# Windowed attention and an affine ResMLP on one core: another order of the first steps

## The chip, the cores and the metric

The kernel runs on one core of a Trainium2 chip. The metric is device time in microseconds (us), lower is better; before the change the median of three runs is 258.79 us (256.25 to 259.25).

## The reference

Two parts follow each other, on float32 inputs. Attention with batch 4, 8 heads, 768 positions, head size 64: a query sees the first 4 positions (sinks) and the 128 latest. Its result is laid out as x (4, 768, 512) and goes through an affine MLP block:

```python
scores = scale * q @ k^T            # kept: sinks or 0 <= rel < 128
x   = softmax(scores) @ v           # heads side by side: (B, S, 512)
a1  = alpha1 * x + beta1
u   = x + lam * (w_tok @ a1)        # w_tok: 768 x 768, over positions
a2  = alpha2 * u + beta2
out = u + lam * (relu(a2 @ w_ch1) @ w_ch2)   # 512 -> 2048 -> 512
```

## The kernel before

The Python code does not issue instructions as it goes. It adds some 1143 small steps to a plan (`add`), each a closure that issues one or a few instructions on one engine. At the end `plan.emit(ORDER, ENGINES, HOMES, IDLES)` runs the steps in the order of the tuple ORDER; the digit string ENGINES gives each step's engine (0 ACT, 1 DVE, 2 PE, 3 POOL, 4 SP), HOMES gives each buffer's place in its pool, and IDLES puts filler matmuls on a zero tile ahead of a step (step, PSUM home, number). So ORDER sets the order on every engine and every DMA queue. Waits come from the data and buffers that instructions share; each engine takes its instructions in the order in which they were issued.

A batch goes through: loading q and k of head pairs, casting to 16 bits, transposing (for the first two batches on PE, L504 and L507, evicted by ACT or DVE, L155 and L157), scores (L617 and L681; for some tiles a bias matmul, L612 and L678, puts the mask in first), exp on ACT, masks on DVE or POOL, the product with v (L718, with the sinks' part at L604 and L711), the norm (L743, L744), then the token mixing (`tok`, L849), u (L856), its transposes (L890), the first matmul of the MLP in 32 groups of four matmuls per batch (`mlp1`, L929), relu (L935, L937), and the second matmul (L1114, or in batches 1 to 3 a Strassen form, L1046). Steps of the next batch's attention are mixed into the MLP of the one before.

What concerns the start:

- SP's queue (`load_qk` L397, `load_v0` L424, `load_wtok` L435) asks for w_tok's first tile, q and k of the first head pair, and then slices of v and further tiles of w_tok. The other head pairs of batch 0 come in as casting DMAs of POOL (L390, into 16 bits). w_ch1 comes in four quarters, also casting DMAs of POOL (`load_w1`, L448); SP has small copies that wait for a quarter (`gate`, L455).
- ScalarE's queue asks for alpha2 and beta2 (`ab_row`, L169, L170), and, after DVE has zeroed their tiles, for lam, alpha1 and beta1, four copies of each row (L192).
- `fold_rows` multiplies alpha1 and beta1 by lam (DVE, L1164), spreads the rows over the partitions with a shuffle (L1166), transposes `ab_row` on PE (`abT`, L1168) and copies it to `ab2`.
- POOL makes the constants: `make_iden` (L325, L326), `make_masks` (L333 to L341), `make_bm` (L358), `make_sel` (L365, L369); DVE makes the biases from the masks (L348). PE's transposes need the identity.
- `cast_wtok` casts a tile of w_tok with its row sums (DVE L816 or ACT L814), transposes it (L809) and evicts it to `wtokT`. `cast_v0` casts batch 0's v.
- POOL forms half products of x with lam*alpha1 (L753), the operand of `tok`.

Of the kernel before, what the change touches and what calls it, by code (L numbers as in the profile page):

```python
# [77 lines left out]
def kernel(  # L78
# [119 lines left out]
    for r in range(NR):  # L198
# [18 lines left out]
        26, 6, 9, 7, 10, 5, 11, 8, 18, 15, 72, 19, 1, 12, 3, 0, 4, 2, 22, 14, 73, 74, 45, 48, 46,  # L217
        17, 39, 49, 47, 53, 13, 40, 50, 41, 90, 95, 43, 91, 51, 54, 103, 52, 16, 44, 61, 104, 42,
        96, 109, 100, 62, 107, 110, 63, 55, 28, 108, 92, 56, 101, 21, 68, 65, 59, 93, 20, 69, 97,
        102, 111, 94, 24, 98, 57, 60, 30, 112, 105, 23, 58, 99, 113, 128, 106, 114, 116, 25, 131,  # L220
        135, 78, 115, 64, 27, 138, 31, 32, 117, 132, 29, 129, 136, 33, 122, 66, 125, 34, 123, 137,
        119, 139, 126, 35, 79, 70, 120, 140, 124, 84, 71, 80, 133, 130, 141, 67, 146, 85, 134, 121,
        147, 144, 75, 118, 158, 86, 154, 148, 159, 145, 142, 87, 149, 150, 155, 160, 143, 76, 88,
        151, 156, 81, 77, 166, 152, 162, 167, 89, 127, 82, 163, 213, 83, 168, 209, 164, 165, 214,
        210, 153, 217, 179, 211, 178, 157, 197, 229, 36, 212, 215, 218, 185, 216, 226, 230, 219,
        176, 161, 177, 220, 169, 223, 222, 232, 225, 224, 221, 227, 237, 233, 279, 238, 234, 228,
        273, 280, 182, 171, 204, 291, 274, 175, 289, 292, 200, 231, 293, 290, 246, 294, 295, 199,
        384, 241, 248, 188, 186, 257, 296, 247, 172, 243, 277, 174, 181, 242, 259, 258, 187, 170,
        278, 267, 37, 260, 271, 358, 268, 198, 285, 349, 272, 381, 301, 286, 366, 351, 303, 302,
        189, 297, 378, 173, 304, 281, 180, 352, 203, 249, 190, 282, 298, 379, 250, 287, 380, 192,  # L230
        353, 385, 288, 206, 283, 386, 369, 375, 367, 265, 284, 368, 202, 370, 266, 363, 376, 371,
        253, 377, 201, 299, 254, 372, 364, 183, 382, 191, 300, 373, 615, 365, 275, 374, 383, 357,
        261, 276, 408, 262, 387, 263, 184, 409, 205, 195, 239, 411, 264, 410, 395, 269, 396, 240,
        397, 270, 196, 388, 614, 621, 235, 412, 400, 194, 244, 398, 236, 401, 255, 617, 251, 245,
        256, 389, 390, 399, 252, 311, 359, 207, 193, 391, 424, 616, 335, 425, 393, 341, 426, 392,
        336, 648, 427, 634, 413, 394, 312, 636, 414, 428, 419, 404, 420, 415, 360, 405, 313, 429,
        208, 422, 337, 416, 361, 441, 421, 622, 402, 314, 423, 442, 626, 403, 305, 638, 315, 406,
        430, 640, 316, 435, 431, 306, 641, 355, 436, 443, 619, 437, 338, 649, 618, 438, 362, 317,
        432, 637, 407, 307, 433, 345, 444, 339, 439, 635, 318, 445, 450, 434, 639, 644, 319, 451,
        628, 452, 620, 440, 308, 645, 340, 453, 417, 446, 323, 447, 418, 320, 309, 448, 324, 321,  # L240
        658, 322, 329, 449, 642, 659, 454, 325, 625, 643, 330, 646, 347, 455, 326, 623, 343, 647,
        464, 344, 456, 465, 348, 466, 460, 457, 467, 650, 327, 458, 331, 461, 629, 459, 472, 462,
        632, 463, 653, 356, 651, 656, 627, 332, 38, 654, 480, 333, 342, 624, 652, 473, 310, 476,
        468, 471, 470, 469, 481, 474, 488, 885, 477, 475, 482, 492, 655, 490, 493, 350, 483, 478,
        514, 491, 516, 489, 657, 479, 515, 660, 517, 630, 882, 665, 518, 663, 354, 328, 666, 502,
        880, 661, 664, 498, 879, 519, 508, 499, 346, 503, 678, 662, 512, 509, 679, 504, 513, 487,
        484, 671, 485, 676, 486, 506, 677, 877, 548, 505, 672, 680, 507, 526, 549, 546, 527, 631,
        334, 522, 674, 681, 528, 547, 907, 523, 534, 903, 529, 633, 682, 675, 878, 542, 683, 535,
        890, 689, 543, 550, 685, 684, 690, 510, 551, 494, 511, 673, 667, 544, 495, 668, 891, 496,
        686, 545, 901, 687, 669, 497, 693, 888, 688, 883, 530, 694, 670, 700, 531, 524, 897, 701,  # L250
        698, 500, 691, 525, 696, 699, 552, 501, 697, 704, 553, 558, 695, 705, 904, 692, 562, 559,
        706, 909, 887, 707, 563, 564, 898, 708, 702, 566, 565, 910, 715, 703, 567, 532, 716, 889,
        713, 533, 709, 714, 896, 520, 710, 556, 717, 521, 538, 557, 537, 540, 539, 536, 560, 541,
        899, 718, 921, 572, 922, 881, 711, 574, 884, 573, 576, 712, 561, 719, 902, 577, 575, 555,
        727, 720, 569, 908, 721, 580, 728, 578, 722, 581, 729, 554, 723, 905, 730, 568, 739, 724,
        579, 725, 592, 570, 911, 726, 582, 740, 593, 588, 912, 583, 595, 584, 571, 906, 743, 589,
        731, 585, 900, 590, 732, 605, 744, 587, 733, 596, 606, 734, 607, 611, 594, 597, 602, 745,
        612, 586, 613, 599, 895, 603, 591, 757, 765, 600, 758, 601, 759, 766, 741, 771, 760, 742,
        916, 772, 751, 917, 746, 773, 752, 913, 761, 919, 774, 886, 767, 918, 604, 762, 763, 598,
        768, 777, 764, 779, 920, 923, 780, 914, 755, 915, 778, 608, 756, 926, 930, 735, 609, 931,  # L260
        924, 927, 781, 736, 925, 775, 782, 737, 928, 753, 929, 893, 738, 934, 754, 892, 769, 935,
        932, 610, 941, 770, 819, 776, 942, 894, 939, 820, 821, 940, 937, 936, 823, 749, 822, 945,
        748, 824, 938, 747, 827, 933, 948, 950, 750, 952, 943, 951, 825, 953, 787, 828, 944, 807,
        788, 797, 826, 808, 949, 946, 829, 798, 801, 954, 830, 791, 802, 956, 947, 792, 783, 955,
        957, 963, 961, 784, 789, 958, 962, 811, 790, 964, 959, 785, 812, 965, 805, 786, 795, 806,
        960, 967, 796, 799, 793, 968, 966, 970, 972, 794, 813, 971, 969, 815, 973, 814, 809, 800,
        816, 803, 810, 974, 978, 804, 976, 979, 837, 975, 977, 835, 838, 980, 841, 836, 839, 842,
        818, 843, 840, 845, 981, 832, 982, 846, 817, 986, 844, 831, 990, 987, 983, 988, 847, 991,
        984, 851, 833, 992, 1002, 993, 834, 848, 855, 852, 985, 849, 1003, 859, 856, 1004, 989,
        1006, 850, 860, 1005, 853, 998, 1007, 1008, 868, 999, 857, 1009, 997, 865, 995, 858, 862,  # L270
        996, 869, 866, 1000, 874, 994, 854, 1001, 1016, 863, 875, 1040, 1017, 1038, 1041, 1032,
        1039, 871, 1020, 872, 1028, 1021, 1011, 1024, 1029, 1013, 1018, 1033, 1012, 1025, 1034,
        1019, 1036, 1010, 1035, 1042, 1037, 1076, 1043, 1070, 1077, 870, 1074, 1071, 1054, 1075,
        1022, 1055, 1060, 1023, 1048, 1061, 1058, 1049, 1066, 1059, 1014, 1044, 1015, 1067, 1072,
        1045, 1056, 1073, 1026, 1057, 1078, 1068, 1079, 1064, 1069, 1046, 1027, 1050, 1063, 1047,
        1052, 1082, 1053, 1051, 1084, 1083, 1062, 1065, 1030, 1085, 1080, 1101, 1031, 1081, 1091,
        1102, 1107, 1092, 1097, 1093, 1103, 864, 1108, 1105, 867, 1098, 1111, 1106, 1104, 1113,
        1112, 1089, 1114, 1115, 1086, 1116, 1090, 861, 1094, 1087, 1117, 1099, 1109, 1100, 1121,
        1095, 1110, 1125, 1118, 1122, 1124, 1134, 1126, 1123, 1128, 1135, 1127, 1119, 1136, 1088,
        1140, 1120, 873, 876, 1131, 1129, 1141, 1096, 1137, 1142, 1132, 1130, 1133, 1138, 1139,  # L280
    )
    ENGINES = (
        "3313134433443333444444444444444433334441111201201202120212021213030121211201211210200200"
        "2020201202011202020202020213213213213213213202002020202020213121312131213121312131404444"
        "4044413314433334411114413334444042213221321021020121021021321202020020211212021212120212"
        "1212020202120202120212020212020202020212122221022221422221022221422221022221013111111131"
        "1311333333302002002102132002132002102020101212010321213120301212131201012121312010121213"
        "1203212131212131213421342104110121042104213401012020202021202020212120202020212120202121"
        "2121202111202021202120202011202121212121111121212121212121132111213121421021421421421044"
# [1033 lines left out]
```

The softmax here doesn't subtract the row's maximum and nothing guards it: scores larger than these inputs give would overflow.

## Time and profile before

The profiled execution has a span of 254.3 us from the first to the last instruction; its own run time is not given apart from the three runs.

| | us |
|---|---|
| runs: median (lowest to highest) | 258.79 (256.25 to 259.25) |
| span of the profiled execution | 254.3 |
| PE busy in it | 245.6 |
| first fillers on PE; first transposes; first scores | 1.06; 7.60; 11.19 |
| first `tok` matmul | 31.39 |
| first `mlp1` matmul | 39.83 |
| issue of w_ch1's four quarters on POOL | 20.96 to 24.0 |
| last matmul | 250.05 |

Busy time counts an engine's instructions from start to end; filler matmuls count as busy too. A time in brackets behind an instruction is how long its engine was idle before it, with what ended that. Engines and lines are named as above; DMA queue q1 is SP's, q10 ScalarE's, q0 POOL's.

### The profile page before, as it was taken

How to read it: one execution, taken by the hardware profiler on the slowest of the kernel's cores; microseconds unless marked ns; L12 is line 12 of the kernel's file. 1: busy time of each engine (PE TensorE's matmuls, PEld its weight loads, DVE VectorE, ACT ScalarE, POOL GpSimd, SP SyncE). 2: the span in 40 equal slices, each digit the busy share in tenths (PEclk: the TensorE clock that was granted, in tenths of full speed). 3: DMA queues.
4: the chain of work that ended last, by engine and by line, in shares of the span. 5: the costliest groups of instructions: out<-in, count | busy, mean ns of one | idle time of the engine just before them, and what ended most of it. 6: DMA issues, size and time to landing. Idle time of an engine off the chain costs nothing.

```text
span 254.3 us, 5499 instructions
## 1 busy us (share of the span) xinstructions
PE 245.6 (97%) x2167; PEld 159.9 (63%) x2167; DVE 190.7 (75%) x402; ACT 133.2 (52%) x219; POOL 103.2 (41%) x124
## 2 busy tenths in 40 slices
PE   7799997999999999999999999999999999999993
PEld 7554644666555544566687686667667676667882
DVE  5688986767888874978879995578778983228892
ACT  2599913879977034787833434566660235543000
POOL 8318845876455527515782040065662120000010
PEclk9999999999999999999999999999999999999998
DMA  6999999899999999998484764520000140100327
GB/s 182 205 215 266 272 269 316 246 377 300 221 158 233 234 208 156 195 249 180 110 170 107 128 122 138 144 65 0 3 0 3 30 84 13 41 0 3 117 73 268
DMA packets 86129, 38.79 MB, mean 153 GB/s; under 512 B 73540, under 2 KB 80460, under 8 KB 86104
## 3 DMA queue, kind: packets, MB, share of 16 engines
q1 hardware_dynamic: 66576, 28.06, 47.3%
q10 hardware_dynamic: 15784, 7.11, 11.8%
q0 software_dynamic: 3744, 3.28, 8.0%
q8 instruction: 17, 0.28, 0.4%
q14 instruction: 8, 0.07, 0.1%
HBM read 29.91 MB, written 6.29 MB: 142 GB/s over the span
## 4 chain that ended last, share of the span: by engine, by line
PE 84%; DMA 11%; DVE 2%; POOL 1%; SPq 0%; issue 0%
PE h L929 32%; PE P L1046 22%; PE tok L849 9%; PE ch L1114 8%; DMA w1f<-in_moe_w_ch_dram 8%; PE pv L718 3%; PE S L617 3%; DMA nat<-in_k_dram 3%; PE tp L507 1%; POOL w1f L448 1%; PE tp L504 1%; DVE qkT L157 1%; DVE E L696 1%; PE pv L711 1%; PE pv L604 1%; PE idle L148 0%
## 5 line engine op out<-in xcount | busy, mean ns | idle before, releaser
L929 PE MATMUL h<-uT,w1f 128*128 128x384 f16 x512 | 89.8, 326 | 1.5 <-DMA w1f<-in_moe_w_ch_dram 1.5
L929 PEld LDWEIGHTS <-w1f 128*128 128x128 f16 x512 | 48.2, 98 | 32.7 <-DMA w1f<-in_moe_w_ch_dram 1.9
L935 ACT ACTIVATE hT<-h 128x384 f16<-128x384 f32 x77 | 37.0, 491 | 39.5 <-PE h L929 39.3
L937 DVE TENSOR_SCALAR hT<-h 128x384 f16<-128x384 f32 x51 | 27.8, 555 | 23.4 <-PE h L929 22.8
L1046 PEld LDWEIGHTS <-hT 128*128 128x128 f16 x408 | 39.5, 98 | 6.7 <-issue 0.2
L639 ACT ACTIVATE E<-S 128x1024 f16<-128x1024 f32 (+1 forms) x39 | 38.1, 1001 | 7.6 <-PE S L617 6.3
L762 POOL TENSOR_TENSOR tm<-x,la_b 128x512 f32<-128x512 f32 x18 | 24.3, 1353 | 24.2 <-DVE x L744 12.3
L849 PE MATMUL tok<-xh,wtokT 128*128 128x512 f16 x144 | 33.0, 379 | 0.0
L1059 DVE TENSOR_TENSOR x<-x,P 128x256 f32<-128x256 f32 x45 | 18.3, 419 | 11.3 <-PE P L1046 10.2
L1046 PE MATMUL P<-w2f,hT 128*128 128x256 f16 x216 | 26.5, 273 | 0.0
L849 PEld LDWEIGHTS <-wtokT 128*128 128x128 f16 x144 | 13.9, 98 | 15.0
L1114 PE MATMUL ch<-w2f,hT 128*128 128x512 f16 x96 | 23.2, 379 | 0.0
L1046 PE MATMUL P<-w2s,hT 128*128 128x256 f16 x192 | 23.1, 273 | 0.0
L1082 POOL TENSOR_TENSOR x<-x,pt 128x256 f32<-128x256 f32 x4 | 3.4, 854 | 47.5 <-DVE pt L1077 47.5
L155 ACT CAST u<-x 128x512 f16<-128x512 f32 x15 | 9.2, 615 | 24.9 <-DVE x L856 24.3
L744 DVE TENSOR_TENSOR x<-pv,rec 128x256 f32<-128x256 f32 x48 | 20.4, 425 | 1.7
L155 ACT CAST n<-nat 128x768 f16<-128x768 f32 x21 | 16.9, 828 | 8.9 <-DVE x L1125 6.4
L718 PEld LDWEIGHTS <-E 128*128 128x128 f16 x328 | 14.8, 98 | 5.1 <-issue 1.1
L856 DVE TENSOR_TENSOR x<-x,tok 128x512 f32<-128x512 f32 x24 | 16.0, 683 | 2.3 <-PE tok L849 2.3
L718 PE MATMUL pv<-vfs,E 128*128 128x65 f16 x328 | 17.7, 194 | 0.0
L579 POOL TENSOR_SCALAR_AFFINE_SELECT E<-E 128x512 f16<-128x512 f16 x12 | 7.5, 648 | 20.6 <-ACT E L639 20.6
L743 DVE RECIPROCAL rec<-pv 128x4 f32<-128x4 f32 x48 | 8.6, 179 | 7.2 <-PE pv L718 6.9
(134 smaller groups left out, 340.6 us busy)
## 6 DMA issues: line engine op xcount, KB each, us to landing
wst_w<-in_moe_w_ch_dram SPq DMA_DIRECT2D x8, 512.0 KB, 8.2
nat<-in_q_dram SPq DMA_DIRECT2D x10, 384.0 KB, 3.9
vnat<-in_v_dram SPq DMA_DIRECT2D x14, 256.0 KB, 5.7
nat<-in_k_dram SPq DMA_DIRECT2D x8, 384.0 KB, 7.2
out_dram<-x SPq DMA_DIRECT2D x11, 256.0 KB, 3.1
out_dram<-x ACTq DMA_DIRECT2D x10, 256.0 KB, 3.7
wtn<-in_moe_w_tok_dram SPq DMA_DIRECT2D x6, 384.0 KB, 4.1
w1f<-in_moe_w_ch_dram POOLq DMA_DIRECT2D x4, 512.0 KB, 15.4
```

Source lines behind the costliest of these rows:

```text
L155: nc.scalar.copy(o, i)
L639: nc.scalar.activation(eT.t, pS.t[:, :, 0 : n * w].rearrange("p e (i w) -> p e i w", i=n), AF.Exp, scale=scale)
L718: nc.tensor.matmul(po.t[:, hl, :], eT.t[:, e_, off + i, c : c + P], vf[j][:, h, :], start=(r < 2 and n == 0), stop=(n == len(parts) - 1 an ...
L744: nc.vector.tensor_mul(bx.t[:, 4 * G : 4 * G + 4, :], po.t[:, :, 0:D], rec.t.to_broadcast([P, 4, D]))
L762: engine[e].tensor_mul(bt.t, bx.t.rearrange("p h d -> p (h d)"), la1_b)
L849: nc.tensor.matmul(pt.t, wtokT[:, si, ti * P : (ti + 1) * P], hs[si].t, start=(si == 0), stop=(si == NR - 1))
L929: nc.tensor.matmul(ph.t, w1f[:, c, fi * P : (fi + 1) * P], bu.t[:, c, chk * NTOK : (chk + 1) * NTOK], start=(c == 0), stop=(c == NC - 1))
L935: nc.scalar.activation(bh.t[:, fi, :], ph.t, AF.Relu)
L937: nc.vector.tensor_scalar_max(bh.t[:, fi, :], ph.t, 0.0)
L1046: nc.tensor.matmul(pc.t, hh[:, nt * P : (nt + 1) * P], w(fi), start=(first and n_ == 0), stop=(n_ == HF - 1), skip_group_check=True)
L1059: nc.vector.tensor_add(row(bx)[:, cols], row(bx)[:, cols], pc.t)
L1114: nc.tensor.matmul(pc.t, bh.t[:, fi, nt * P : (nt + 1) * P], w2f[:, fi, :], start=(fi == 0), stop=(fi == NF - 1))
```

## The change

No step is added or removed, and no closure is altered: ORDER, ENGINES, HOMES and IDLES are replaced. Read as queues, batch 0's start changes thus:

- SP: q and k of the first pair go ahead of w_tok's first tile; the rest keeps its order.
- POOL: make_sel goes ahead of the first casting DMA; make_iden ahead of make_masks; make_bm behind the last two casting DMAs of q and k; w_ch1's first quarter goes directly behind the first v cast, the other three directly behind the second, all ahead of the first half product. POOL also gets two v casts (from ACT and DVE), and some half products change places.
- DVE: the product lam*beta1 comes first, then the casts of q and k, the product lam*alpha1, the copy to ab2 (from ACT), alpha1's shuffle, the biases, the eviction of the first k transposes (from ACT), the cast of w_tok's first tile, the eviction of the second pair's k (from ACT), the copy into vs, and the eviction of w_tok's first transposes (from ACT). beta1's shuffle comes later.
- ACT: evicts the second pair's q and the fourth pair's k (from DVE), and casts w_tok's tile 2 in place of tile 4.
- PE: abT first, then 52 fillers, transposes of q and k, the first two score tiles, transposes of the second pair's k, of w_tok's first tile, the third score tile, transposes of the second pair's q. Before: w_tok's transposes, those of q, k and the second pair's k, two score tiles, abT, the second pair's q, the third score tile.
- `mlp1` of batch 0, first half: before, the groups ran 1, 11, 8, 13, 12, 14, (uT transposes), 15, (uT transposes), 4, 10, 5; after, 1, 11, 8, 4, 10, 5, (both uT transposes), 15, 13, 14, 12. Groups 12 to 15 read w_ch1's last quarter, 4 to 7 its second, 8 to 11 its third.
- About a dozen steps behind that change engine (relu between ACT and DVE, casts of w_ch2 and sums between DVE and POOL), and some buffers change homes. Most of the order from batch 1 on is as before.

```diff
     ORDER = (
-        26, 6, 9, 7, 10, 5, 11, 8, 18, 15, 72, 19, 1, 12, 3, 0, 4, 2, 22, 14, 73, 74, 45, 48, 46,
-        17, 39, 49, 47, 53, 13, 40, 50, 41, 90, 95, 43, 91, 51, 54, 103, 52, 16, 44, 61, 104, 42,
...
+        6, 7, 5, 26, 9, 43, 10, 11, 8, 18, 15, 41, 0, 45, 1, 48, 19, 39, 46, 44, 12, 22, 49,
+        17, 40, 14, 2, 13, 50, 16, 3, 47, 90, 72, 95, 53, 96, 91, 54, 73, 103, 4, 51, 74,
+        28, 52, 61, 104, 100, 62, 109, 63, 32, 21, 107, 110, 20, 24, 55, 108, 101, 30, 56,
...
     ENGINES = (
-        "3313134433443333444444444444444433334441111201201202120212021213030121211201211210200200"
+        "3313134433443333444444444444444433334441111211201212021212021203330321211211210210201200"
...
     IDLES = (
-        (73, 0, 65), (46, 0, 12), (49, 1, 1), (90, 3, 10), (61, 3, 2), (109, 3, 3), (92, 3, 1),
-        (166, 1, 4), (162, 0, 1),
+        (46, 0, 52), (90, 3, 10), (61, 3, 2), (109, 3, 3), (92, 3, 1), (166, 1, 4), (162, 0,
+        1),
     )
```

Numbers in it, for the steps named here: 0 iden, 1 masks, 2 bias, 3 bm, 4 copy into vs, 5 sel; 6, 7 loads of q and k of the first pair; 8, 9 and 12 to 15 casting DMAs of the other pairs; 26 load of w_tok's first tile; 32 to 35 w_ch1's quarters; 39, 40 alpha1's product and shuffle, 41, 42 those of beta1; 43, 44 abT and its copy; 45, 46, 47 cast, transposes and eviction of the first q, 48, 49, 50 those of the first k; 51 to 54 transposes and evictions of the second pair; 61, 62 of the fourth pair's k; 72, 73, 74 cast, transposes and eviction of w_tok's first tile; 90, 95, 103, 109 score tiles.

## The prediction

> **What bounds the kernel now.** I read the page first, then the table of windows, then the timelines of PE and DVE, then the chain of waits, then the DMA queues by window. The page's first part:
>
> ```profile
> PE 245.6 (97%) x2167; PEld 159.9 (63%) x2167; DVE 190.7 (75%) x402; ACT 133.2 (52%) x219; POOL 103.2 (41%) x124
> ```
>
> The windows (length, then busy time of PE, PEld, DVE, ACT, POOL; clock, DMA share, GB/s):
>
> ```profile
> 11.19:13.54 2.35, 2.35 (x41) 1.50 (x39) 1.63 (x4) 2.03 (x5) 0.61 (x1) 1.00 1.29 213
> 13.54:31.40 17.86, 17.80 (x240) 9.70 (x238) 15.87 (x41) 16.92 (x28) 11.01 (x15) 1.00 1.05 251
> 31.40:41.95 10.55, 10.54 (x63) 5.24 (x60) 9.00 (x16) 3.77 (x7) 4.06 (x7) 1.00 1.16 278
> 41.95:43.45 1.50, 0.00 (x1) 0.01 (x1) 0.56 (x1) 0.00 (x0) 1.50 (x2) 1.00 1.08 385
> 43.45:250.05 206.60, 206.59 (x1715) 135.81 (x1715) 156.47 (x315) 106.81 (x177) 78.51 (x81) 1.00 0.60 132
> ```
>
> From 11.19 us, the first scores, PE has one hole, 1.50 us; after 43.45 it has none until its last matmul. So a change early in the kernel moves the end by just two things: when PE's full stretch starts, and whether the hole stays. PE's timeline says what the hole is and where the stretch starts (start, length, what):
>
> ```profile
> 7.60 0.49 PE L809 MATMUL wT<-iden,wt 128*128 128x128 f16 x6 [1.50 <-POOL iden L326]
> ...
> 11.19 0.39 PE L681 MATMUL S<-qkT 64*128 64x256 f16 x4
> ...
> 13.54 0.59 PE L612 MATMUL S<-biasn,iden 128*128 128x512 f16 x2
> ...
> 43.45 2.12 PE L929 MATMUL h<-uT,w1f 128*128 128x384 f16 x12 [1.50 <-DMA w1f<-in_moe_w_ch_dram]
> ```
>
> The chain of waits has the same hole as the end of one transfer, the last quarter of w_ch1:
>
> ```profile
> 23.23 20.17 DMA w1f<-in_moe_w_ch_dram
> ```
>
> What feeds 11.19 is on DVE:
>
> ```profile
> 3.82 0.95 DVE L816 TENSOR_SCALAR_CACHE_REDUCE wt<-wtn 128x768 f16<-128x768 f32 x1 [0.23 <-DMA wtn<-in_moe_w_tok_dram]
> ...
> 8.13 0.56 DVE L157 CAST n<-nat 128x768 f16<-128x768 f32 x1 [0.51 <-PE wT L809]
> 9.01 0.56 DVE L157 CAST n<-nat 128x768 f16<-128x768 f32 x1 [0.31 <-DMA nat<-in_k_dram]
> 9.48 0.69 DVE L1164 TENSOR_TENSOR la_b<-la_b,lam_r 128x512 f32<-128x512 f32 x1
> ...
> 10.84 0.67 DVE L1164 TENSOR_TENSOR lb_b<-lb_b,lam_r 128x512 f32<-128x512 f32 x1
> 12.23 0.96 DVE L157 COPY qkT<-tp 128x768 f16<-128x768 f16 x1 [0.72 <-PE tp L504]
> ```
>
> q is cast at 8.13, k at 9.01 as it lands; after that the row products lam*alpha1 (9.48) and lam*beta1 (10.84). ScalarE's DMAs for those rows leave at 2.33, 2.98 and 3.58, but the DMA queue of ScalarE (q10) has no packet from 3.75 to 6.25; all 24 of the three rows fall into 6.25 to 9.35, and later there are none up to 12:
>
> ```profile
> q10 hardware_dynamic: 24, 0.02, 3.4%
> ```
>
> In finer windows its last packet is at 9.10 to 9.35: the last row, beta1's, is in SBUF at about 9.35, unseen because its reader comes at 10.84.
>
> **What the Trainium skill says.** "Trainium Architecture — The Big Picture", Inside one NeuronCore: each engine runs its own instruction stream and meets the others at semaphores. The 7.06 us start of DVE's copy behind its 2.28 us wait for POOL, with q long landed (issued at 1.27, 3.5 us to landing), agrees: what stands behind a waiting instruction waits too. "DMA: Bandwidth & Descriptors", Issuing engines are not separate DMA queues: transfers of all engines run on the same 16 DMA engines and interleave. The 8 KB rows that take over 4 us agree. "TensorE: Matmul & The Clock Gate", What's actually happening: the clock halves after an idle window of about 3.4 us. Here the granted clock is 1.00 in all windows above; no run shows a fall.
>
> **The change part by part.** T is the landing of the beta1 row.
>
> 1. DVE's order. Before: cast of w_tok's first tile, copy into vs, biases, q, k, alpha1's product. After: beta1's product is first, then q, k, alpha1's product, the copy of ab2, alpha1's shuffle, biases, then the eviction of k's transposes (moved from ACT). So q and k, asked for one place earlier on SP (0.4 us, and ahead of 384 KB), may land at about 4 and 5 us and then stand behind beta1's row. From starts in DVE's timeline: product 0.58 to the next start; q cast 0.47; k cast 0.47; product 0.69; copy about 0.1 (128x8, bounded by the 0.19 of the like copy into vs); shuffle 0.63; biases 0.14 + 0.27. The eviction starts near T + 3.3 and takes 0.96; scores follow 0.22 later (10.97 to 11.19 before): T + 4.5.
>
> 2. PE's order. Before, w_tok's transposes and those of the second k pair came ahead of the scores; now they come after (0.33 + 0.46 us), and the abT transpose (about 0.15) goes first; the fillers (65 at the start, 12 and 1 between the transposes) become 52 behind abT. w_tok's cast follows the eviction on DVE (0.88 + 0.08): its transposes start at T + 5.15. Then 0.33, scores with bias 0.53, transposes of the second q pair 0.46, those of a fourth-pair k with 2 fillers 0.6, 3 fillers; the eviction of the second q pair, now on ACT (0.80), ends at T + 7.4. The scores that stood at 13.54 start at T + 7.45: the stretch shifts by T − 6.09.
>
> 3. T. What is queued ahead of ScalarE's rows is the same: q, k, w_tok's tile and the first v slices, in another order. POOL's first cast DMA now goes out behind make_sel (0.54 + 0.19 us), so the cast DMAs' queue, 21.4% of the DMA time in 3.75 to 6.25, starts about 1.1 us later and leaves up to 0.5 us. T is between 8.85 and 9.35 if nothing else moves; below 6.1 the part would gain. I take 8.9: shift +2.81.
>
> 4. Fourth quarter of w_ch1. Its groups move behind three groups of the second quarter (3 x 4 x 0.163 = 1.95 us) and two uT transposes (0.67). PE would reach it at 41.95 + 2.6 + 2.8 = 47.4, and it landed at 43.4 even when issued last. The hole goes: −1.50. The three groups' own quarter landed by 36 (gate at 35.96).
>
> 5. POOL. identity ahead of masks: needed at 10 now, made near 5.2; free. The third cast DMA of k waits for the k cast (T + 1.6 = 10.5 instead of 9.57), 6.7 us to landing, used near 20: free. w_ch1's first quarter goes out behind the first v cast (13.5 instead of 20.96), the others at about 17.7: no longer behind a half product. They share the DMA from 16.3. With both queues busy q1 moved 0.1 MB in 0.5 us at 24 to 27, against 0.14 alone at 18 to 22; the remaining 2.1 MB of v and w_tok end near 28.5 instead of 26.2. Its last reader, a cast at 29.76, is itself 2.8 later. Free, with 4 us of cover; without cover it costs one for one.
>
> 6. Casts and copies that change engine: ACT gives one v cast (0.62) and takes a net 0; POOL takes two v casts (0.6 and about 0.9) and has lost 3.05 us of issues from the same stretch; DVE loses 0.95. PE is full there, so none of it gains, and POOL's last half product (32.87) still ends before its reader, which moves to 35.9. SBUF and PSUM homes: renamed, no wait found. The engine swaps behind 43.45 have no idle PE to win back: 0, with ±0.5.
>
> Sum on the profiled execution: 254.3 + 2.81 − 1.50 = 255.6 us. Runs lie at 256.25 to 259.25, 2 to 5 us above that span; its own run time is not given apart. On the median: 258.79 + 1.31 = **260.1 us**.
>
> **Rivals.**
> A. As above: DVE's head wait takes the place of the hole. T from 7.5 to 9.4 gives −0.1 to +1.8: 258.7 to 260.6. For: the q10 line. Chance 0.52.
> B. The rows land early (the change as it seems meant): T = 5.6 gives −0.5, with the hole −2.0: 256.8. For: 8 KB is little, and k and q no longer stand behind w_tok. Against: the rows' packets began when v's small ones did, and everything ahead of them is still ahead. Even T = 4 only gives −3.6, since PE's work must be done. Chance 0.22.
> C. Slower: the clock. From about 8.2 (52 fillers behind abT at about 3.7) to 13.4 PE has only some 1.2 us of work. If its clock halves there, a 3.4 us window costs 1.7: 261.8. Beyond 2% it needs 2 x (5.2 − 1.3) = 7.8 us at half clock; three windows (10.2 us) give 265.2. Against: PE before paused 1.5 us with no drop. Chance 0.14.
> D. w_tok late: if w_ch1's quarters ran at their lone rate (0.1 MB in 0.5 us) and q1 stood still for 10.5 us, w_tok would end at 34.3, 2.0 past its reader: 262.1. Against: the queues share evenly at 30 to 36. Chance 0.12.
>
> **How the numbers follow.** About 2%, 5.2 us, is what a measurement here can tell from no change. A, B and most of C and D lie inside; only the long form of C, and a second mishap on D, pass it: slower 0.14, faster 0.04 (B's best does not reach it; run scatter might), same 0.82. Range: 256.3, below B, to 263.3, above C and D in their short form.
>
> **What would show it.** Step 1: beta1's product first on DVE with a wait on its DMA until 8 to 9.4, scores at 13 to 14. Wrong if it starts before 7. Steps 2 and 3: bias scores at T + 7.45. Step 4: no PE wait for w1f, however late. Step 5: no wait of a cast for w_tok beyond about 1 us. C: a clock under 1.00, or matmuls at double spacing, between 10 and 18.

## The result and the profile after

The changed kernel takes 265.74 us (median of six runs, 264.43 to 268.59), the kernel before 258.19 us (six runs, 256.25 to 259.25). The ratio is 1.0317, with a 95% interval of [1.0271, 1.0364]: slower by 3.2%, beyond the range of the prediction. Some executions of these kernels are disturbed and one or two per cent longer, as the longest of the six is; the ratios here and below leave them out, the medians do not. The profiled execution took 265.73 us with a span of 262.9 us, so 2.8 us lie around its span.

The page's first part, as it was shown of before:

```profile
PE 247.8 (94%) x2141; PEld 161.1 (61%) x2141; DVE 192.3 (73%) x399; ACT 132.0 (50%) x216; POOL 110.5 (42%) x130
```

PE has 26 instructions less, which are fillers, and 2.2 us more busy time; the span has grown by 8.6. So PE now stands idle for part of the time, or works slowly. The windows (length, then busy time of PE, PEld, DVE, ACT, POOL; clock, DMA share, GB/s), cut at the bias scores that the prediction calls the start of PE's full stretch, and at the first `tok` matmul:

```profile
16.57:28.80 12.23, 11.89 (x150) 5.71 (x147) 7.33 (x18) 11.71 (x19) 3.44 (x5) 1.00 1.20 219
28.80:30.60 1.80, 0.00 (x0) 0.00 (x0) 1.00 (x3) 1.02 (x1) 0.00 (x0) 1.00 1.21 199
30.60:37.40 6.80, 5.47 (x52) 3.33 (x53) 3.03 (x10) 2.41 (x5) 4.20 (x6) 0.51 0.89 291
37.40:39.93 2.53, 2.42 (x41) 1.85 (x38) 2.28 (x8) 2.46 (x4) 1.60 (x4) 0.98 0.58 180
39.93:53.00 13.07, 13.07 (x87) 7.18 (x85) 11.20 (x21) 5.12 (x10) 6.82 (x8) 1.00 0.65 205
```

The second and third rows are new: a stretch of 1.80 us without one matmul, and behind it 6.8 us at a granted clock of 0.51, with 52 matmuls where the same time held about 91 before (240 in 17.86 us). PE's timeline (start, length, what; in brackets the idle time ahead and what ended it) says what was missing:

```profile
13.30 0.39 PE L686 MATMUL S<-qkT 64*128 64x256 f16 x4 [1.40 <-DVE qkT L157]
...
16.57 0.59 PE L617 MATMUL S<-biasn,iden 128*128 128x512 f16 x2
...
30.62 0.79 PE L814 MATMUL wT<-iden,wt 128*128 128x128 f16 x6 [1.85 <-DVE wt L821]
...
34.07 0.98 PE L723 MATMUL pv<-vfs,E 128*128 128x65 f16 x15 [1.31 <-POOL vfs L157]
...
39.93 6.71 PE L854 MATMUL tok<-xh,wtokT 128*128 128x512 f16 x30
```

A cast of w_tok (`wt`) and a cast of v (`vfs`) came late. (Lines of this kernel are numbered 5 higher than before's: L854 is `tok`, L821 the cast of w_tok.) What these casts waited for is on DVE, ACT and POOL:

```profile
29.60 0.95 DVE L821 TENSOR_SCALAR_CACHE_REDUCE wt<-wtn 128x768 f16<-128x768 f32 x1 [2.54 <-DMA wtn<-in_moe_w_tok_dram]
```

```profile
35.00 0.84 ACT L819 ACTIVATE wt<-wtn 128x768 f16<-128x768 f32 x1 [1.98 <-DMA wtn<-in_moe_w_tok_dram]
```

```profile
33.20 0.83 POOL L157 CAST vfs<-v 128x768 f16<-128x768 f32 x1 [6.94 <-DMA v<-in_v_dram]
```

And the chain of waits, which before had w_ch1's last quarter as its long transfer, now has a slice of v, issued at 18.67 and landed 14.38 us later:

```profile
18.67 14.38 DMA v<-in_v_dram
```

Where the 8.6 us are, from the two profiled executions (last matmul ends at 250.04 before, 258.62 after):

| stretch | before | after | difference |
|---|---|---|---|
| start to the first bias scores | 13.54 | 16.57 | +3.03 |
| bias scores to the first `tok` matmul | 17.85 | 23.36 | +5.51 |
| the wait for w_ch1's last quarter | 1.50 | 0 | −1.50 |
| first `tok` to the last matmul, without that wait | 217.15 | 218.69 | +1.54 |

These are two single executions. The medians lie 7.55 us apart and the spans 8.6, and the start alone scatters by about a microsecond: a kernel told of below, in which only MLP groups are moved, has the start of the kernel before unchanged, and in its trace the bias scores start at 14.73 instead of 13.54.

### The profile page after: what moved, and what is told of

It is laid out like the page before. It is cut to its first block, busy times and chain, and to the rows that moved or that the text cites. A ratio compares the mean times of both kernels' runs of the same rounds, so it can differ in the third digit from the quotient of the medians.

```text
span 262.9 us, 5460 instructions
## 1 busy us (share of the span) xinstructions
PE 247.8 (94%) x2141; PEld 161.1 (61%) x2141; DVE 192.3 (73%) x399; ACT 132.0 (50%) x216; POOL 110.5 (42%) x130
## 4 chain that ended last, share of the span: by engine, by line
PE 80%; DMA 7%; DVE 5%; SPq 4%; issue 1%; POOL 0%; DVEq 0%; POOLq 0%
PE h L934 29%; PE P L1051 20%; PE tok L854 12%; PE ch L1119 8%; DMA v<-in_v_dram 5%; PE pv L723 4%; SPq L429 3%; PE S L622 3%; DMA lam_r<-in_moe_lam_dram 2%; DVE hS L992 1%; SPq L440 1%; DVE w2f L836 1%; PE tp L512 1%; DVE hT L942 1%; PE pv L716 1%
## 5 line engine op out<-in xcount | busy, mean ns | idle before, releaser
L767 POOL TENSOR_TENSOR tm<-x,la_b 128x512 f32<-128x512 f32 x18 | 24.9, 1382 | 21.8 <-DVE x L749 12.9
L854 PE MATMUL tok<-xh,wtokT 128*128 128x512 f16 x144 | 33.1, 379 | 0.0
L854 PEld LDWEIGHTS <-wtokT 128*128 128x128 f16 x144 | 14.0, 98 | 14.9 <-issue 0.2
L723 PEld LDWEIGHTS <-E 128*128 128x128 f16 x328 | 15.8, 100 | 7.5 <-issue 3.7
L723 PE MATMUL pv<-vfs,E 128*128 128x65 f16 x328 | 18.7, 198 | 1.3 <-POOL vfs L157 1.3
L584 POOL TENSOR_SCALAR_AFFINE_SELECT E<-E 128x512 f16<-128x512 f16 x12 | 8.9, 765 | 17.9 <-ACT E L644 17.9
```

The lines of the kernel that those rows point to most:

```text
L723: nc.tensor.matmul(po.t[:, hl, :], eT.t[:, e_, off + i, c : c + P], vf[j][:, h, :], start=(r < 2 and n == 0), stop=(n == len(parts) - 1 an ...
L767: engine[e].tensor_mul(bt.t, bx.t.rearrange("p h d -> p (h d)"), la1_b)
L854: nc.tensor.matmul(pt.t, wtokT[:, si, ti * P : (ti + 1) * P], hs[si].t, start=(si == 0), stop=(si == NR - 1))
```

## The experiments

They are told in groups. Each ratio is to the kernel before, measured beside it. The diffs are cut down to the steps that move, with some neighbours.

**Is it w_ch1 beside v and w_tok, or the late start?** Two edits of the changed kernel, each alone: w_ch1 issued late again, or beta1's product taken out of the first place on DVE.

```diff
 # w_ch1 late
-        62, 109, 63, 32, 21, 107, ... 113, 33, 105, ... 114, 34, 31, ... 135, 35, 42, ... 117, 130, 125,
+        62, 109, 63, 21, 107, ... 113, 105, ... 114, 31, ... 135, 42, ... 117, 130, 32, 33, 34, 35, 125,
 # beta1's product later
-        6, 7, 5, 26, 9, 43, 10, 11, 8, 18, 15, 41, 0, 45, ... 17, 40, 14,
+        6, 7, 5, 26, 9, 43, 10, 11, 8, 18, 15, 0, 45, ... 17, 40, 41, 14,
```

> The changed kernel with w_ch1's four quarters issued on POOL behind the first half product, as in the kernel before; nothing else moved. Theory P (the early quarters starve SP's queue, whose v slices are 256-byte packets served one for one with w_ch1's): the waits for v (6.9 us on POOL) and w_tok (2.5 and 2.0 us) go, the clock stays at 1.00, the first tok matmul comes at 34.4 (31.4 before plus the 3.0 of the head), no w1f hole, span 256 to 257.5, time about 260 to 261, about 1% over before. Theory H (the late head, DVE behind beta1's row, is the cause of most of the 8 us): the time stays near 265.

> The changed kernel with only beta1's product moved on DVE from first place to behind alpha1's shuffle. Casts of q and k then start when q lands, near 4 us. Theory P: the stall for v ends at the same time by the clock (33 us), so tok starts at 39 to 40 as in the changed kernel and the time falls by less than 1 us (264.5 to 266). Theory H: the head's 3 us come back, about 262.5. In both the first transposes wait for the 52 fillers, which end at 10.0, so first scores come at about 12 rather than 13.3.

With w_ch1 late the time falls to 260.66 us, ratio 1.0136 [1.0032, 1.0239]. The three waits of casts shown above are gone (POOL keeps two short ones for v, 1.17 and 1.31 us before 16 us, where the kernel before has 2.27 and 3.55), the clock stays near full (0.997 over the span), and `tok` starts at 34.69 instead of 39.93:

```profile
34.69 6.75 PE L854 MATMUL tok<-xh,wtokT 128*128 128x512 f16 x30
```

From the bias scores (16.52) to `tok` this is 18.17 us, against 23.36 in the changed kernel and 17.85 before. So 5.2 of the 5.51 us in the table belong to the early w_ch1. The queues in 17 to 24 us (packets, MB, share of the 16 engines' time), the changed kernel first, then this one:

```profile
q0 software_dynamic: 1078, 1.08, 90.9%
q1 hardware_dynamic: 1163, 0.31, 30.2%
```

```profile
q1 hardware_dynamic: 2576, 2.05, 97.3%
```

In the same 7 us SP's queue q1 moved 2.05 MB alone and 0.31 MB beside w_ch1. Both columns count: alone it sent 368 packets per us, beside w_ch1 166, and its packets there were v's small ones (0.27 KB in the mean, against 0.8 KB alone, where it had got on to w_tok). Between 19 and 20 us, with almost nothing but v's small packets, q1 alone sent 782 of them, 0.23 MB in 1 us; beside w_ch1 it moved 0.044 MB per us.

With beta1's product later, q is cast at 4.01, k at 5.05, and the first scores start at 11.89 instead of 13.30. Still the time is 266.5 us, 1.0362 [1.0277, 1.0447], no better than the changed kernel, where a gain of up to 1 us was expected; `tok` starts at 40.70. PE waits the longer for the transfers:

```profile
32.29 0.82 PE L814 MATMUL wT<-iden,wt 128*128 128x128 f16 x6 [4.30 <-DVE wt L821]
```

The gain at the start was also only 1.4 us, since DVE then waits for alpha1's row, and k's eviction (10.89) stands behind that:

```profile
8.66 0.69 DVE L1169 TENSOR_TENSOR la_b<-la_b,lam_r 128x512 f32<-128x512 f32 x1 [3.06 <-DMA la_b<-in_moe_alpha_dram]
```

**Both edits together.**

> Both edits: w_ch1's quarters behind the first half product, beta1's product behind alpha1's shuffle. Both theories: stall gone and head earlier by about 1.3 us than with the first edit alone; span 255 to 256, time 259 to 260. If the fillers did not bind it would be about 257.

258.57 us over 20 runs, 1.0048 [1.002, 1.0076]; first scores at 12.12, `tok` at 33.59. Once the stall is gone, the earlier start may be worth something: the ratio falls from 1.0136 to 1.0048 and `tok` starts 1.1 us earlier. But the two intervals overlap, and two executions of one start differ by as much, so the gain is not shown. `tok` is still 2.2 us later than before, and something is also lost behind it: from `tok` to the last matmul takes 218.84 us, 1.69 more than before without its hole, which is gone here too.

**The same move in the kernel before.** Only the quarters of w_ch1 are issued early, nothing else of the change is made.

```diff
-        96, 109, 100, 62, 107, 110, 63, 55, ... 68, 65, 59, ... 31, 32, 117, ... 136, 33, 122, 66, 125, 34, ... 126, 35, 79,
+        96, 109, 100, 62, 107, 110, 63, 32, 55, ... 68, 65, 33, 34, 35, 59, ... 31, 117, ... 136, 122, 66, 125, ... 126, 79,
```

> The kernel before with only w_ch1's quarters moved as in the change (first behind the first v cast, the others behind the second). Theory P: POOL, DVE or ACT wait for v and w_tok, tok starts at 35 to 37 instead of 31.4, the w1f hole of 1.5 us goes, span 257 to 259, time 261 to 263.5. Theory H: only the hole goes, time 256.5 to 257.

265.34 us, 1.0324 [1.0204, 1.0443]: more than was expected, and as much as the whole change. `tok` starts at 42.30 (31.39 before), with the bias scores at 13.41 (13.54 before); the hole of 1.50 is gone, the clock is 0.972 over the span. The first of these lines is DVE's, the second PE's, and both have the same cause, a slice of v:

```profile
33.80 0.95 DVE L157 CAST vfs<-v 128x768 f16<-128x768 f32 x1 [5.67 <-DMA v<-in_v_dram]
```

```profile
35.36 0.39 PE L711 MATMUL pv<-vs,es 64*128 64x260 f16 x1 [4.03 <-DVE x L744]
```

DVE's norm, for which PE waits, stands behind the cast of v in DVE's order.

**Bytes or packets?** Beside w_ch1, q1 fell to 0.31 MB in 7 us, which an even split of bytes would not give. v is read in runs of 64 floats, 256 bytes, and the packets of q0 carry 1 KB each. If the queues take turns packet by packet, larger packets of v should mend it with w_ch1 still early. The edit of `load_v0` in the changed kernel:

```diff
-                bf.t[:, sl], v[0, 4 * G : 4 * G + 4, r * P : (r + 1) * P, :].rearrange("h p d -> p h d")),
+                bf.t[:, sl].rearrange("p h d -> p (h d)"), v[0, 4 * G : 4 * G + 4].rearrange("h s d -> (h s d)")[r * P * 4 * D : (r + 1) * P * 4 * D].rearrange("(p f) -> p f", p=P)),
```

> The changed kernel, with batch 0's v slices read as flat stretches of the same size in runs of 1 KB instead of 256 B; v's elements thus come in a wrong order, which is the part of the computation that it changes. Same bytes, a quarter of the packets. Theory P (one packet of SP's queue is served for each packet of w_ch1's): q1 moves four times the bytes beside w_ch1, the v cast on POOL and the w_tok casts wait for no more than 1 us, tok starts near 34.4 to 35, span 256 to 258, time about 260. Rival B (the queues share by bytes or time, and w_ch1's 2 MB simply cannot fit ahead of v and w_tok): the stalls stay, time 264 to 266.

This kernel leaves out the right placing of batch 0's v, so its output is not the reference's; the steps and the bytes are the same. 259.85 us over 18 runs, 1.0106 [1.008, 1.0131]: w_ch1 is as early as in the changed kernel (from 11.78, there from 12.82), and the stall is gone. POOL's cast of v, which had stood until 33.20, has no wait in brackets now:

```profile
25.60 0.82 POOL L157 CAST vfs<-v 128x768 f16<-128x768 f32 x1
```

The queues in 17 to 21 us:

```profile
q0 software_dynamic: 429, 0.43, 63.6%
q1 hardware_dynamic: 430, 0.65, 52.2%
```

Packets are nearly equal again, as they were in the changed kernel (1078 and 1163) and with the same move in the kernel before (893 and 885 in 24 to 30), and now a packet of q1 is worth more. `tok` starts at 33.87, so that from the bias scores (15.97) to `tok` it takes 17.90 us. The kernel with w_ch1 late has 18.17, by a quite different edit: it takes both, w_ch1 early and v in small packets, to make the stall. What larger packets save on the DMA engines by themselves was not separated from this; the equal counts speak for turns.

**What the low clock costs.** In the changed kernel, fillers are put into the stall, so that PE is at work while it waits.

```diff
     IDLES = (
-        (46, 0, 52), (90, 3, 10), (61, 3, 2), (109, 3, 3), (92, 3, 1), (166, 1, 4), (162, 0, 1),
+        (46, 0, 52), (90, 3, 10), (61, 3, 2), (109, 3, 3), (92, 3, 1), (85, 1, 30), (158, 2, 26), (166, 1, 4), (162, 0, 1),
     )
```

> The changed kernel with 30 filler matmuls ahead of w_tok's tile-4 transposes and 26 ahead of the fourth row's product with v, where PE stands still. If the halved clock costs what its length says (7 us at 0.50 after the stall, about 3.3 us of them with work), the clock stays at 1.00, tok starts 1 to 1.7 us earlier (38.2 to 39) and the time is about 264.5. If PE waits for others there anyway, the time stays within 0.5 us of the changed kernel's.

The clock stays at 1.00, where the changed kernel had 0.51:

```profile
30.60:37.40 6.80, 6.05 (x93) 4.32 (x91) 4.42 (x15) 3.30 (x6) 3.87 (x6) 1.00 0.88 286
```

Bias scores to `tok` take 22.2 us instead of 23.36 (16.79 to 39.02). The time is 264.47 us, 1.027 [1.0213, 1.0327], an interval that overlaps that of the changed kernel. So the clock has about 1.1 of the 5.5 us in the trace, which the time does not resolve; the late data have the rest.

**What is lost behind `tok`.** In the changed kernel PE waits until 144.30, for 0.76 us, for two differences on DVE (hS, operands of the Strassen form); they run there beside a POOL addition. DVE, then POOL, then PE of the changed kernel:

```profile
140.53 3.72 DVE L992 TENSOR_TENSOR hS<-hT,hT 128x1536 f16<-128x1536 f16 x2
```

```profile
141.55 1.87 POOL L770 TENSOR_TENSOR xh<-tm,lb_b 128x512 f16<-128x512 f32 x1
```

```profile
144.30 1.92 PE L1051 MATMUL P<-w2f,hS 128*128 128x256 f16 x16 [0.76 <-DVE hS L992]
```

The next kernel is the one with both edits, with step 718, that POOL addition, put back on DVE, where the kernel before has it, and behind the differences.

```diff
-        538, 557, 718, 540, ... 711, 899, 921,
+        538, 557, 540, ... 711, 899, 718, 921,
 # ENGINES, step 718: 3 (POOL) to 1 (DVE)
```

> The third kernel (quarters late, beta1's product later) with one step of batch 2, the sum into xh (row 5), back on DVE from POOL, behind batch 2's Strassen difference. Theory: DVE's differences (3.71 us for two, 2.64 before) are stretched by POOL's float32 work beside them; the 0.75 us hole at 138 goes, span about 256.0, time 0.7 below the third kernel. Rival: the hole comes from the order alone and stays.

257.93 us over 20 runs, 1.0035 [1.0007, 1.0063], against 258.57 (1.0048) without it. The intervals overlap, so the time does not show the gain, but the trace is plain: the hole is gone, and the differences take 2.63 us:

```profile
134.00 2.63 DVE L992 TENSOR_TENSOR hS<-hT,hT 128x1536 f16<-128x1536 f16 x2
```

Even that is not their time with POOL at rest. Taken singly, the first difference lasts 1.76 us here and in the changed kernel, beside a product of POOL; the second lasts 2.03 us in the changed kernel beside the addition and 0.95 here. The profile also shows w_ch1's last quarter 0.70 us late (at 46.75), so that moving the groups does not cover every start of those transfers.

**The good part alone.** In the kernel before, only the groups 12 to 15 of `mlp1` (steps 257 to 296) are moved as the change moves them, with its five relu engines and four PSUM homes there.

```diff
-        171, 204, 291, 274, 175, 289, 292, 200, 231, 293, 290, 246, 294, 295, 199, 384, ... 187, 170, 278, 267, 37, 260, 271,
+        171, 204, 257, 274, 175, 277, 258, 200, 231, 259, 278, 246, 260, 241, 199, 384, ... 187, 170, 290, 267, 37, 294, 271,
 # ENGINES: steps 258 and 290 from DVE to ACT; 278, 292 and 296 from ACT to DVE
```

> The kernel before with only the order of the first MLP groups of batch 0 as in the change (12 to 15 last), with their PSUM homes and relu engines. The hole of 1.5 us goes and nothing else changes: span 252.8, time 0.994 of before. If the hole returns elsewhere (relu, uT), the ratio is 1.00.

256.01 us over 22 runs, 0.9928 [0.99, 0.9955]: faster than both kernels. From the first `tok` to the last matmul it takes 217.41 us (218.65 before): of the 1.50, 1.24 is won, and 0.28 is lost again to one wait for a relu:

```profile
49.15 4.71 PE L929 MATMUL h<-uT,w1f 128*128 128x384 f16 x28 [0.28 <-DVE hT L937]
```

With the later order of the changed kernel the same stretch takes 218.69.

**Can the change's start be made to gain?** Three kernels put the change's first 174 steps, with w_ch1 late and beta1's product later, ahead of the order of the last kernel: with 24 start fillers, with 52, and with all the row work (39, 40, 41) behind the first scores on DVE and other fillers.

```diff
 # the first 174 steps from the changed kernel, w_ch1 behind 130, 41 behind 40; from there on the last kernel's order
 # first: IDLES (46, 0, 24) in place of (46, 0, 52);  second: (46, 0, 52)
 # third: steps 39, 40, 41 moved behind 100, and
+        (43, 1, 48), (90, 3, 10), (53, 2, 16), (51, 1, 8), (61, 3, 6), (109, 3, 3), (92, 3, 1), (166, 1, 4), (162, 0, 1),
```

> A kernel put together: the changed kernel's first 174 steps (with w_ch1's quarters behind the first half product, beta1's product behind alpha1's shuffle, and 24 fillers instead of 52 ahead of q's transposes), then the kernel before with its MLP groups moved (the eighth kernel). q and k are cast by 6.2, fillers end near 7.0, first scores near 9.5 instead of 11 to 12. If the casting DMAs of the other pairs keep pace, tok starts near 31.5 and the time is 0.985 to 0.990 of before; if they (landing at 9 to 11) or a cold clock bind, it is no better than the eighth kernel's 0.993.

> The same kernel with the 52 fillers. They end near 10, so first scores come at 11 to 12, tok at 33, and the time is near 0.993 to 0.998 of before. Its distance to the ninth kernel is what 28 cold fillers cost.

> The ninth kernel with both row products and alpha1's shuffle behind the sinks' copy on DVE, and the fillers put at the very start (48 ahead of abT) and between the first steps. q and k are cast by 5.6, transposed by 6.5, first scores at 8 to 8.5 (11.4 in the ninth and tenth kernels, where k's eviction stands behind alpha1's row). The second pairs' casting DMAs (9 to 11) bind next: bias scores at 12 to 12.5 instead of 14.7, tok at 30.5 to 31.5, time 0.982 to 0.988 of before. If the rows were not the wall, first scores stay at 11 and the time near 0.993.

The first takes 258.34 us, 1.0053 [1.0028, 1.0078], and misses what was expected: k's eviction stands behind alpha1's row (product at 8.22, eviction at 10.43), the scores start at 11.44, and with fewer fillers PE works at little more than half speed until about 17 (ten fillers take 1.27 us there, 0.72 in the changed kernel), so that `tok` starts at 34.97. The second takes 257.68 us, 1.0012 [0.9987, 1.0037], `tok` at 32.85; it too falls short of what was expected. The third takes 255.6 us, 0.997 [0.9951, 0.9989], where 0.982 to 0.988 was expected. With no row ahead of k's eviction its first scores start at 8.41, 4.9 us before the changed kernel's. Its fillers differ too, but the other two kernels start at 11.4 with 24 fillers as with 52, so it was the rows that held the first scores back there. But its bias scores start at 13.40, where before's start:

```profile
8.41 0.39 PE L681 MATMUL S<-qkT 64*128 64x256 f16 x4 [0.77 <-DVE qkT L157]
...
13.40 0.59 PE L612 MATMUL S<-biasn,iden 128*128 128x512 f16 x2
```

The time between holds the later pairs' transposes and 33 fillers. In this trace the second pair's q has landed at about 9.7 and is transposed at 11.87, directly behind eight fillers; a kernel without those fillers was not run, so what holds the bias scores back stays open. An early first pair thus shows no gain over the kernel with nothing but the groups moved: 0.997 here, 0.9928 there (255.6 and 256.01 us, measured at different times, so that differences of half a per cent between the two say nothing).

**One quarter early.** The kernel with only the groups moved, and w_ch1's first quarter alone issued early.

```diff
-        62, 107, 110, 63, 55, ... 138, 31, 32, 117,
+        62, 107, 110, 63, 32, 55, ... 138, 31, 117,
```

> The eighth kernel (before, with the MLP groups moved) with only w_ch1's first quarter issued early, behind the first v cast; the other three stay where they were. The quarter is about 512 packets, so served one for one it holds SP's queue back by some 512 packets, about 3 us at 160 a microsecond, where four quarters held it back by 8 to 10. Theory P: tok 0 to 3 us later than in the eighth kernel, time between 0.993 and 1.003 of before. If any early quarter were enough for the whole stall, it would be near 1.03.

260.13 us, 1.0105 [1.0027, 1.0183], which is some 1.8% above the kernel without the edit (1.0105 / 0.9928) and more than was expected. Its profiled execution was the shortest of its six runs (257.02), so its trace shows less than the median has: bias scores to `tok` take 20.17 us (13.43 to 33.60; 17.85 before), with casts that wait 1.7 and 1.2 us for w_tok. A quarter of the early bytes is already dear; how dear, these few runs leave open.

## Why the prediction was wrong

**Steps 1 to 3, the head: right, more closely than could be expected.** beta1's product is first on DVE and stands until 9.14; the prediction took 8.9, from 8.85 to 9.35:

```profile
9.14 0.69 DVE L1169 TENSOR_TENSOR lb_b<-lb_b,lam_r 128x512 f32<-128x512 f32 x1 [5.54 <-DMA lb_b<-in_moe_beta_dram]
9.75 1.02 DVE L157 CAST n<-nat 128x768 f16<-128x768 f32 x2
```

The bias scores start at 16.57, the rule T + 7.45 gives 16.59; the first scores at 13.30, T + 4.5 gives 13.64, so that two errors of 0.3 us cancel on the way. The shift was predicted as 2.81 and is 3.03; with a start that scatters by about 1 us, so close a hit is partly luck. Rival B, rows that land early, fell by the same line.

**Step 4, the hole: right.** No wait for w_ch1 is left in the changed kernel, and −1.50 is in the account. The groups moved alone (0.9928) show it as a gain of time.

**Step 5 failed: "Free, with 4 us of cover".** The stretch that it put at nothing is 5.51 us longer, of 8.58 in all; 5.2 of this goes away with w_ch1 issued late. The rate of q1 beside w_ch1 was taken as 0.1 MB in 0.5 us, from 24 to 27 us of the kernel before:

```profile
q0 software_dynamic: 261, 0.27, 55.8%
q1 hardware_dynamic: 211, 0.58, 55.3%
```

Read with the packets, the row would have warned: 211 packets of q1 carry 0.58 MB, 2.7 KB each, because these are w_tok's rows of 3 KB. The stretch from 30 to 36 us, from which the prediction took that "the queues share evenly" (rival D, against), is plainer still:

```profile
q0 software_dynamic: 580, 0.58, 56.7%
q1 hardware_dynamic: 573, 1.11, 55.5%
```

The packets are even there, the bytes are not. In the stretch to which the rate was applied, q1 has v's slices too, 256 bytes to a packet. After the change, q1 got 166 packets per us and q0 154, so q1 moved 0.31 MB in 7 us, 0.044 MB per us, where the step reckoned with 0.2. What was true of packets was used as if of bytes. The kernel with v in 1 KB packets shows the cause: same bytes, same order, no stall. The rate itself fits turns: a packet of w_ch1 took an engine 94 ns (90.9% of 16 engines over 7 us, for 1078 packets), so 16 engines pass about 170 of them in 1 us and, taking turns, about as many of v's. That is an estimate; 154 and 166 were measured. The overlap was also longer than reckoned, since the last three quarters went out from 15.07 and not at 17.7. The Trainium skill has the rule: "DMA: Bandwidth & Descriptors", Queues, rings and completion order, says that each DMA engine takes turns between the queues at the granularity of packets. The page's packet holds some 9 to 17 descriptors, and no run here shows that the profile counts the same unit; but the profile's own packets come out nearly even (1078 to 1163, 429 to 430). The prediction did not use it.

Behind v, in SP's order, stands w_tok, so both were late, and each cast that waited held up what follows it on its engine. Rival D had the place and its sign, w_tok past its reader, with 12% and 2.0 us. It had w_tok end at 34.3, and a cast did wait for w_tok until 35.00; its rate for q1, none while w_ch1 ran, was nearer the truth than step 5's. But it left out that v is late with w_tok, and what comes after a stall.

**Rival C** put a fall of the clock into the head. There the changed kernel has none from 11 us on: its first scores take 0.39 us as before, and ten fillers 72 ns each. That the fear was not idle the spliced kernel with 24 fillers shows, in which PE is slow up to 17 us. In the changed kernel the fall came behind the stall instead: PE stood still from 28.77 to 30.62, and the clock was near half from 30.65 to 37.55. It costs about 1.1 us in the trace. The Trainium skill's "TensorE: Matmul & The Clock Gate", What's actually happening, which the prediction named, has the halved clock after an idle window of about 3.4 us. Here it follows one hole of 1.85 us, and with fillers in that hole it does not come; the measurement decides.

**Step 6, "0, with ±0.5": too small.** Behind `tok`, +1.54 without the hole. Of it 0.76 is the wait at 144.30, 0.32 a wait for a relu at 75.22 and 0.10 another at 56.5, where hT stands behind a w2f product on DVE. The first is caused by an engine swap: the POOL addition slows DVE's two differences from 2.63 to 3.72 us, as the kernel with that addition on DVE shows. The Trainium skill's "Trainium Architecture — The Big Picture", What this means for kernel authors, says that DVE and GpSimd contend for a shared pair of ports, held as a lock. The single instructions fit it: the second difference starts at 142.21, the addition ends at 143.42, and the difference ends 0.82 us behind that, where a whole one takes 0.95 with POOL at rest. The other two waits were read from the trace and not tested, and the remaining 0.36 us, in which PE does not stand idle, stays open. That the change's order behind `tok` is to blame the spliced kernels show: with the order of the kernel before, its groups moved, they take 217.6 us there.

The sum with the measured sizes is 3.03 + 5.51 − 1.50 + 1.54 = 8.58. The prediction had 1.31; of the missing 7.3, 5.5 are in step 5 and 1.5 in step 6.

## What to carry to other kernels

Before a transfer is moved ahead beside another queue, count packets in that very stretch, not bytes. Here a queue that reads in 256-byte runs moved 0.31 MB beside one with 1 KB packets, where it moved 2.05 MB alone, and it is the readers of the slowed queue that must be priced. A rate read from a trace holds for the packet size of that row. When a change has several parts, run each alone: here one part (the order of the MLP groups) gains 0.7% and beats both kernels, and another (w_ch1 early) loses 3.2% on its own.

## What the runs showed of the hardware

In the stretches shown two busy queues were served packet for packet: 154 and 166 per us in the changed kernel, whatever the size of a packet. One issue on SP itself lasted 7.1 us while the slices of v asked for ahead of it were still under way; the first issue of a tile of w_tok in the kernel before lasted 0.40. The timeline of SP in the changed kernel:

```profile
19.22 7.10 SPq L440 DMA_DIRECT2D wtn<-in_moe_w_tok_dram  x1
```

The 52 start fillers of the changed kernel take 5.73 us, 110 ns each, and 10 fillers later 72 ns each, while the clock column reads 1.00 over both; so that column does not show the slow start. Nor does it with 24 start fillers, where ten later ones take 127 ns each. And an f16 difference on DVE went from 0.95 to 2.03 us beside a POOL addition that itself went from 1.27 to 1.87 us.
